# Normalizing two tiles on ScalarE in the head and issuing the next block's x loads earlier, in a fused layernorm, state-space and MLP kernel

## The chip, the cores and the metric

One core of a Trainium2 chip. The metric is the device time of one execution in microseconds (us). Each execution also records the span of the core (first to last instruction, about 1.3 us less than the time) and the clock granted to TensorE. All ratios here are the mean time of one kernel's fast runs over that of the other's fast runs of the same rounds, so not quite the ratio of the medians that are quoted. Runs of one call share a chip, and only runs of one call are compared directly unless the text says so.

## The reference, cut to what matters

```python
x  = A_x                                   # [1, 2048, 1024] bf16
xn = layernorm(x)                          # no gain, no bias, eps 1e-5
y  = 2 * Re(C @ scan(Lam_bar, xn @ B_bar)) + xn * Dskip      # 1024 complex states
h  = xn @ w1 + b1                          # w1 [1024, 3584]
z  = (h * tanh(softplus(h))) @ w2          # w2 [3584, 1024]
out = x + y + z
```

## The kernel before

The sequence is cut into four blocks of 512 rows. Each block runs 28 tiles of 128 columns of w1 (numbered 0 to 27 here, eight matmuls each), then the B projection, then a tail with w2 and C. A recording layer notes what each instruction reads and writes and makes the waits; each engine executes its own list in order. In the code PE, VE, AC and PO stand for the lists of TensorE, VectorE, ScalarE and GpSimd, SP for the sync queue, on which most transfers are issued; `mv` holds the mean of a row, `root(q)` one over its standard deviation, and GF is 7. Tile f uses PSUM bank f mod 8, so tile f waits until VectorE has evicted tile f - 8; the B projection starts with banks 4 and 5, those of tiles 20 and 21.

In block 0 the first seven tiles ("raw" tiles) start before x is normalized: rows 0 to 255 go in raw, and the normalization is applied to the product afterwards (`raw_scale`, `raw_add`). Rows 256 to 511 are normalized and transposed first, and `first_rest` (L558) adds them. Weights come through a ring of seven slots of half a K each:

```python
def first_apply(q):                        # normalize 128 rows, all four on VectorE
    vop(lambda e: e.tensor_scalar(xn[:, q, :], xx[:, 0, q, :], mv[:, q, 0:1], root(q),
                                  op0=ALU.subtract, op1=ALU.mult), ...)
...
for f in range(4): first_raw(f, 0, NK // 2)          # PE order of the head
first_spread()                                       # (a transpose of the parameters before it)
for f in range(4): first_raw(f, NK // 2, NK)         # needs the second weight load, "w1" below
...                                                  # statistics of rows 256.. on VectorE
first_sqrt(3)
first_raw(4, 0, NK // 2); first_raw(5, 0, NK // 2)
first_transpose(2); first_copy(2, AC)                # square root of 3 is AHEAD of this copy
first_raw(4, NK // 2, NK); first_raw(5, NK // 2, NK)
...
first_apply(3); first_transpose(3); first_copy(3, VE)
first_raw(6)
...
turns()
for j in range(NJ):                        # GpSimd: eight phases, about 5 us each
    phases(j)
    if j == 3:
        for q in range(NQ):
            load_x(PO, 1, q)               # x of block 1, four loads of 256 KB from GpSimd's queue
...
def first_tile(blk, f):                    # [cut: the eight matmuls]
    if f % 4 == 3:
        item_done(); item_done()           # two weight loads on the sync queue
    if f % GF == 0 and f >= 2 * GF:
        mish_mul(f // GF - 2)              # VectorE, L730: act * hb, 128 x 3584
    vop(...)                               # VectorE, L754: evict the tile
...
if f in (14, 16, 18, 20):                  # block 0, after the tile's eviction
    ln_stats_only(1, (f - 14) // 2)        # VectorE, L449: statistics of block 1's x
if f < 24 and f % 3 == 2:
    transpose_B(f // 3)                    # two transposing DMAs on the sync queue
```

## Time and profile before

| | before |
|---|---|
| median of three timed runs | 620.77 us (620.4 to 621.11) |
| the run whose profile was taken | 623.69 us, span 622.36 |
| TensorE matmul busy | 616.7 us, 99% |
| VectorE busy | 468.1 us, 75% |
| largest TensorE wait after the start-up | 1.8 us, first matmuls of the B projection (L767), for VectorE's eviction |
| VectorE's wait for block 1's x | 3.3 us in two pieces |

In the lines of the profile, here and in the prediction, PE is TensorE's matmuls, PEld its weight loads, DVE VectorE, ACT ScalarE, POOL GpSimd and SPq the issue of a transfer on the sync queue; a line of a timeline gives the start, the duration, the instruction and, in brackets, how long the engine had been idle and what ended that. How to read the rest: the share of busy time says only that TensorE is full; what can be won is in the gaps between its matmuls, and for each gap one asks which wait ends it. The lines are in the prediction. The changed kernel has line numbers about five higher (L754 becomes L759, L767 becomes L772, L449 becomes L454, L730 becomes L735).

### The profile page before, as it was taken

The numbers are of one execution on the slowest core, as the hardware profiler recorded it, in microseconds if no ns is written. First come the engines' busy times: TensorE is split into PE (matmuls) and PEld (weight loads), VectorE is DVE, ScalarE is ACT, GpSimd is POOL, SyncE is SP. The second block draws the span as 40 slices with busy tenths as digits, with TensorE's granted clock in tenths as the row PEclk, the third lists the DMA queues.
The fourth block names the chain that finished last, engine by engine and source line by source line (L and its number), as shares of the span: only waits on it lengthen the run. The fifth ranks groups of instructions, "written<-read, shape, count | busy, mean of one in ns | idle before, by whom it ended". The sixth has DMA issues, their size and how long they took to land.

```text
span 622.4 us, 7428 instructions
## 1 busy us (share of the span) xinstructions
PE 616.7 (99%) x2959; PEld 288.3 (46%) x2959; DVE 468.1 (75%) x698; ACT 248.1 (40%) x161; POOL 54.5 (9%) x57
## 2 busy tenths in 40 slices
PE   8998999999999999999999999999999999999998
PEld 7643444444444444444444444444444444444444
DVE  6988999999557599999047759999624856999603
ACT  4589997332069950000008992000000999000000
POOL 2899200000100000000010000000000000000000
DMA  9999995850355400774054430276302541033001
GB/s 230 298 263 280 224 145 176 199 167 0 117 173 174 144 2 9 218 185 131 11 188 138 135 136 1 73 203 173 93 35 101 164 174 69 1 119 118 1 0 68
DMA packets 97918, 79.94 MB, mean 128 GB/s; under 512 B 51035, under 2 KB 80347, under 8 KB 97883
## 3 DMA queue, kind: packets, MB, share of 16 engines
q1 hardware_dynamic: 94384, 72.17, 41.4%
q0 software_dynamic: 960, 3.15, 1.8%
q10 hardware_dynamic: 2538, 4.14, 1.8%
q8 instruction: 24, 0.39, 0.3%
q14 instruction: 12, 0.09, 0.1%
HBM read 63.19 MB, written 4.19 MB: 108 GB/s over the span
## 4 chain that ended last, share of the span: by engine, by line
PE 90%; POOL 4%; DMA 2%; DVE 2%; issue 1%; SPq 0%; POOLq 0%; DVEq 0%
PE ps L825 49%; PE ps L745 23%; PE ps L767 18%; DMA xx<-in_A_x_dram 2%; POOL py L627 1%; POOL px L625 1%; POOL ph_h L629 1%; DVE stats L449 1%; POOL rb L568 1%; DVE hb L754 1%; DVE act L730 0%; PE ps L839 0%; DVE stats L371 0%; SPq L310 0%; SPq L343 0%
## 5 line engine op out<-in xcount | busy, mean ns | idle before, releaser
L825 PE MATMUL ps<-ring,act 128*128 128x512 bf16 x896 | 194.0, 379 | 0.0
L745 PE MATMUL ps<-xnT,ring 128*128 128x512 bf16 x840 | 182.1, 379 | 0.0
L723 ACT ACTIVATE act<-hb 128x3584 bf16<-128x3584 bf16 x16 | 50.9, 3183 | 220.6 <-DVE hb L754 220.1
L825 PEld LDWEIGHTS ps<-ring,act 128*128 128x128 bf16 x896 | 87.7, 98 | 105.7
L745 PEld LDWEIGHTS ps<-xnT,ring 128*128 128x128 bf16 x840 | 82.1, 98 | 99.2 <-DVE hb L754 0.7
L754 DVE TENSOR_SCALAR hb<-ps,par 128x512 bf16<-128x512 f32 (+1 forms) x112 | 80.0, 730 | 52.6 <-PE ps L745 51.7
L767 PE MATMUL ps<-xnT,BT 128*128 128x512 bf16 x512 | 111.3, 379 | 1.8 <-DVE hb L754 1.8
L825 PE MATMUL ps<-CT,hT 128*128 128x512 bf16 x506 | 109.9, 379 | 0.0
L772 DVE TENSOR_TENSOR mt<-ps,tab 128x1024 bf16<-128x1024 f32 x64 | 75.4, 1219 | 13.3 <-PE ps L767 11.7
L767 PEld LDWEIGHTS ps<-xnT,BT 128*128 128x128 bf16 x512 | 50.0, 98 | 62.5 <-DVE hb L754 2.3
L825 PEld LDWEIGHTS ps<-CT,hT 128*128 128x128 bf16 x506 | 49.5, 98 | 59.7
L790 DVE TENSOR_TENSOR_SCAN hT<-cs,qi,hT 128x512 bf16<-128x512 f32 x48 | 58.9, 1269 | 0.0
L870 DVE TENSOR_TENSOR xx<-ps,xx 128x1024 bf16<-128x1024 f32 (+1 forms) x16 | 18.8, 1190 | 45.6 <-PE ps L825 45.6
L725 ACT ACTIVATE act<-act 128x3584 bf16<-128x3584 bf16 x16 | 51.1, 3191 | 0.2
L724 ACT ACTIVATE act<-act 128x3584 bf16<-128x3584 bf16 x16 | 51.0, 3190 | 0.2
L795 DVE TENSOR_TENSOR mt<-hT,tab 128x1024 bf16<-128x1024 bf16 x64 | 41.4, 688 | 1.1
L730 DVE TENSOR_TENSOR act<-act,hb 128x3584 bf16<-128x3584 bf16 x16 | 34.0, 2127 | 1.3 <-ACT act L725 1.3
L310 POOL DMA_DIRECT2D xx<-in_A_x_dram x12 | 6.7, 562 | 250.2 <-DVE xx L870 245.8
L699 ACT ACTIVATE ct<-CT,cs 128x512 f32<-128x512 bf16 x16 | 11.5, 720 | 26.3 <-DVE CT L701 25.9
L725 ACT ACT_TABLE_LOAD x16 | 20.5, 1283 | 0.3
L724 ACT ACT_TABLE_LOAD x16 | 20.5, 1283 | 0.3
L449 DVE BATCH_NORM_STATS2 stats<-xx 128x6 f32<-128x512 bf16 x24 | 16.3, 679 | 3.7 <-DMA xx<-in_A_x_dram 3.3
(101 smaller groups left out, 297.9 us busy)
## 6 DMA issues: line engine op xcount, KB each, us to landing
ring<-in_B_w_dram SPq DMA_DIRECT2D x112, 512.0 KB, 4.1
out_dram<-xx ACTq DMA_DIRECT2D x15, 256.0 KB, 2.0
xx<-in_A_x_dram POOLq DMA_DIRECT2D x12, 256.0 KB, 4.2
xx<-in_A_x_dram SPq DMA_DIRECT2D x3, 256.0 KB, 4.7
xx<-in_A_x_dram SPq DMA_DIRECT2D x2, 128.0 KB, 2.3
dsk<-in_A_Dskip_dram SPq DMA_DIRECT2D x1, 256.0 KB, 5.1
xnT<-xn SPq DMA_TRANSPOSE x14, 4.5
BT<-in_A_B_re_dram SPq DMA_TRANSPOSE x8, 5.8
```

Of the source, the lines that this page charges most:

```text
L449: vop(lambda e, h=h: e.bn_stats(stats[:, s, h, :], xx[:, i, q, h * 512:(h + 1) * 512]), reads=[b_xx[i][q]], writes=[b_stats[s]])
L723: aop(lambda e: e.activation(a, hs, AF.Exp), reads=[b_hb[g % 2]], writes=[b_act[g]])
L724: aop(lambda e: e.activation(a, a, AF.Ln, bias=1.0), reads=[b_act[g]], writes=[b_act[g]])
L725: aop(lambda e: e.activation(a, a, AF.Tanh), reads=[b_act[g]], writes=[b_act[g]])
L730: vop(lambda e: e.tensor_tensor(a, a, hs, op=ALU.mult), reads=[b_act[g], b_hb[g % 2]], writes=[b_act[g]])
L745: PE.mm(lambda e, k=k, w=w: e.matmul(ps[:, bank, :], lhsT=w, rhs=xnT[:, k, :], start=k == 0, stop=k == NK - 1), reads=[b_ring[s]] + b_xnT, ...
L754: vop(lambda e: e.tensor_scalar(hb[:, hs, ts], ps[:, bank, ts], b1(f), None, op0=ALU.add), reads=[b_ps[bank], b_par], writes=[b_hbf[hs]])
L767: PE.mm(lambda e, j=j, ci=ci, k=k, bank=bank: e.matmul(ps[:, bank + ci, :], lhsT=BT[:, ci, j, k, :], rhs=xnT[:, k, :], start=k == 0, stop= ...
L772: vop(lambda e, s=s, u=u, j=j: e.tensor_tensor(mt[:, s, :, :], u, tab[:, s, j, :].unsqueeze(1).to_broadcast([P, 2, TB]), op=ALU.mult), rea ...
L790: vop(lambda e, ci=ci, init=init: e.tensor_tensor_scan(out=hT[:, ci, j, :], data0=cj("r", j).to_broadcast([P, TB]), data1=hT[:, ci, j, :], ...
L795: vop(lambda e, s=s: e.tensor_tensor(mt[:, s, :, :], hT[:, :, j, :], tab[:, s, j, :].unsqueeze(1).to_broadcast([P, 2, TB]), op=ALU.mult), ...
L825: PE.mm(lambda e: e.matmul(ps[:, u, :], lhsT=lhsT, rhs=rhs, start=st_, stop=last), reads=reads, writes=[b_ps[u]], first=st_, last=last)
```

## The change

Two changes joined. First, in the head, the normalization of rows 0 to 255 moves from VectorE to ScalarE (their transposes into xnT are not needed before tile 7), the raw tiles 4, 5 and 6 run all first halves and then all second halves, the transpose of the parameters moves behind the second halves of tiles 0 to 3, tile 2's copy is cut in two, and one more weight load is issued at once. Second, the x loads of block 1 are issued after phase 1 instead of phase 3, so that VectorE does not wait for them.

```diff
     def first_apply(q):
+        if q < 2:
+            aop(lambda e: e.activation(xn[:, q, :], xx[:, 0, q, :], AF.Identity,
+                                       bias=rr[:, 2 + q:3 + q], scale=root(q)), ...)
+            return
         vop(lambda e: e.tensor_scalar(xn[:, q, :], ...
 ...
     def bank_T(q, k):
-        if q < 2 and k >= NK // 2:
-            return 4 + q
-        return 6 + q % 2
+        if q < 2:
+            return 4 + q + 2 * (k < NK // 2)
+        return 7
 ...                                        [cut: sign of the column sums, csum for ncs]
     first_scale(2)
     first_apply(2)
     first_sums_v(3, 1)
     first_var_v(3)
+    first_transpose(2)
+    first_copy(2, AC, 0, 4)
     first_sqrt(3)
-    first_raw(4, 0, NK // 2)
-    first_raw(5, 0, NK // 2)
-    first_transpose(2)
-    first_copy(2, AC)
-    first_raw(4, NK // 2, NK)
-    first_raw(5, NK // 2, NK)
+    first_copy(2, AC, 4, NK)
     raw_scale(0)
+    for f in range(4, NR):
+        first_raw(f, 0, NK // 2)
     first_scale(3)
     first_apply(3)
     first_transpose(3)
     raw_scale(1)
     first_copy(3, VE)
-    first_raw(6)
+    for f in range(4, NR):
+        first_raw(f, NK // 2, NK)
+    for q in range(2):
+        transpose_dma(q)                   [moved here; the fifth weight load now goes ahead of it]
 ...
     for j in range(NJ):
         phases(j)
-        if j == 3:
+        if j == 1:
             for q in range(NQ):
                 load_x(PO, 1, q)
```

## The prediction

> **What bounds the kernel now.** I first read the page's busy shares, then the waits, then the chain that ended last in order of time, then two stretches of the timeline: 7 to 17 us (the head) and 40 to 66 us (where the chain changes hands). Page of the kernel before:
>
> ```profile
> PE 616.7 (99%) x2959; PEld 288.3 (46%) x2959; DVE 468.1 (75%) x698; ACT 248.1 (40%) x161; POOL 54.5 (9%) x57
> ...
> PE   8998999999999999999999999999999999999998
> PEld 7643444444444444444444444444444444444444
> DVE  6988999999557599999047759999624856999603
> ```
>
> TensorE matmuls fill 99% of the span, so only a gap between matmuls can be won. Which gaps exist:
>
> ```profile
> DVE stats L449 <- DMA xx<-in_A_x_dram: 3.3, 2, 2.5
> ...
> PE ps L767 <- DVE hb L754: 1.8, 1, 1.8
> ...
> PEld ps L549 <- DMA ring<-in_B_w_dram: 1.1, 2, 0.7
> ...
> PEld ps L745 <- DVE hb L754: 0.7, 2, 0.5
> ```
>
> Apart from the start-up these are the only TensorE waits worth the name: one big one where the B projection (L767) begins, and small ones in the head. Chain that ended last, in order of time:
>
> ```profile
> 42.16 0.69 POOL xx L310
> 42.85 8.25 DMA xx<-in_A_x_dram
> 51.10 0.02 issue
> 51.12 0.71 DVE stats L449
> ...
> 58.48 2.96 DVE act L730
> ...
> 61.54 0.76 DVE hb L754
> ...
> 62.35 26.07 PE ps L767 x120
> ```
>
> Until 62.35 us the end is set by other engines: GpSimd's phases, the load of the next block's x, VectorE. From 62.35 to the end it is TensorE nearly without break; going through the starts of its matmuls I find none that starts more than 0.24 us after the one before. So the time is "when does matmul 9 of L767 start" plus a constant 560 us. The stretch 40 to 66 us:
>
> ```profile
> 47.41 1.43 DVE L449 BATCH_NORM_STATS2 stats<-xx 128x6 f32<-128x512 bf16 x2 [2.51 <-DMA xx<-in_A_x_dram]
> ...
> 58.40 3.03 DVE L730 TENSOR_TENSOR act<-act,hb 128x3584 bf16<-128x3584 bf16 x1
> ...
> 61.54 4.70 DVE L754 TENSOR_SCALAR hb<-ps,par 128x512 bf16<-128x512 f32 x7
> ```
>
> VectorE, in program order, sits idle 2.51 and then 0.78 us for x, falls behind, and evicts tile 21 (bank 5) only at 61.54 to 62.29. TensorE's matmul before the gap starts at 60.17, the next at 62.35: 2.18 us against a normal pitch of 0.216, a loss of 1.96. Another 0.15 is lost at 53.10 (tile 25 waiting for the eviction of tile 17). Head:
>
> ```profile
> 7.76 5.81 SPq L489 DMA_TRANSPOSE xnT<-xn  x2
> ...
> 11.79 0.55 DVE L383 TENSOR_SCALAR xn<-xx,mv,rs 128x1024 bf16<-128x1024 bf16 x1
> ...
> 13.22 0.29 ACT L379 ACTIVATE rs<-mv,kon 128x1 f32<-128x1 f32 x1 [2.54 <-DVE ncs L564]
> ...
> 13.74 0.55 DVE L383 TENSOR_SCALAR xn<-xx,mv,rs 128x1024 bf16<-128x1024 bf16 x1
> 13.96 1.01 ACT L412 COPY xnT<-ps 128x1024 bf16<-128x1024 bf16 x1 [0.45 <-PE ps L401]
> ```
>
> Here the square root of tile 3 (13.22) runs before the copy of tile 2 (13.96); the change swaps them.
>
> **What the Trainium skill says.** "Perfetto Trace Analysis", section Optimization Strategy: take the regime, find the gaps of its most-contended engine and what they wait for. That is the reading above, and the trace supports it. "ScalarE: Activation LUTs", section What ACT_TABLE_LOAD costs: an ACTIVATE with immediates takes 186 ns + 0.833 ns per element, each [128,1] pointer operand adds about 93 ns. The trace agrees: 1039 ns by the formula, 1012 measured for the 1024-wide copy. So a ScalarE normalization, with two pointers, is estimated at 1.23 us, where VectorE took 0.55. The same page, section Table sets, says that identity is in every set; the instruction listings have 40 ScalarE entries with a table load before and 40 after, so no load is added. "DMA: Bandwidth & Descriptors", section Queues, rings and completion order: each DMA engine consumes descriptors in ring order. The trace agrees in the head: issue order x1, w0, x2, w1, x3, w2, w3 lands at 5.24, 6.67, 7.33, 10.26, 10.97, 12.36, 13.77. A fifth weight load issued behind w3 should delay none of these.
>
> **The change, part by part.**
>
> *x loads two phases sooner.* GpSimd issues the four loads after phase 1 (its end is at about 31.3) instead of after phase 3 (42.1): 10.8 us sooner. The first two landed 5.3 and 9.0 us after the issue began (47.4, 51.1), so I expect about 37 and 41. VectorE asks first at 44.89, then after one tile's statistics and two evictions, 1.64 + 1.36 = 3.0 us later, at 47.9. Both idle times, 3.29 us, go. Tile 21 is then evicted by 62.29 - 3.29 = 59.0. TensorE would reach it, without gaps, at 58.66 - 0.15 + 8 x 0.216 = 60.24: slack 1.2 us, so both losses go whole, 1.96 + 0.15 = 2.1 us, and 1.2 us of VectorE's gain is worth nothing. GpSimd's total work, and so the end of phase 7 (66.3), stays.
>
> *The head.* Two normalizations (2 x 0.55 us) leave VectorE; this gains it nothing, as its next statistics of tile 3 wait for x3 (10.97) in either version, and the normalization of tile 2 ends at 12.34 as before. TensorE does the same matmuls in another order: raw at 0.112 us pitch, transposes at 0.056. Second halves of tiles 0 to 3 begin with w1 at 10.31 again and end at 12.10; the parameter transpose to 12.2; transposes of tile 2 wait for 12.34, so start at 12.39 and leave at 12.90; twelve first-half matmuls (12 x 0.112) end at 14.25. ScalarE starts half of tile 2's copy 0.25 after its last transpose, at 13.03; the square root of tile 3 follows 0.48 later (the pitch of the 512-wide copies in the head), at 13.51, against 13.22. Reciprocal and normalization follow at the old distances (+0.33, +0.20, +0.55): xn of tile 3 at 14.58, and its transposes start at 14.64, a gap of 0.39. They leave at 15.15; twelve second-half matmuls end at 16.5. VectorE's copy of tile 3 runs 15.28 to 15.97 and is hidden. So L558, the remainder of the raw tiles, starts at 16.5, against 16.11: a **loss of 0.4 us**. The order saves the old waits for w2 (0.30) and for the copy (0.06) and puts a wait for tile 2 (0.2) and one for tile 3 (0.39) in their place, besides small shifts.
>
> *The two transposes by DMA and the fifth weight load.* xn of tile 1 comes from ScalarE at about 11.7 instead of 8.8, so I estimate landings at 17 to 19 instead of 16.15 and 17.0. They are needed at tile 7, 22.6: hidden. w4 comes sooner, needed at 24: hidden.
>
> Sum: 2.1 - 0.4 = 1.7 us. From 62.35 on nothing changes: 620.77 - 1.7 = 619.1.
>
> **Rivals.**
> 1. *The head gains.* VectorE freed and w3 undisturbed by the transposes might bring TensorE's remainder forward to 15.8. For it: two waits of the old head do vanish. Against it: x3 and w1 fix 10.31 and 12.34 regardless. It would give 618.4.
> 2. *The gap of 1.96 turns into another wait,* since VectorE has 1.2 us of slack: tile 21's eviction stands behind the 3.03 us multiplication L730, which needs ScalarE's tanh (50.45 + 3.19 = 53.64). VectorE reaches it at 55.1, so it is not held. If the loads came later than I think (DMA is saturated here, busy share about 1.1), half of the gap would stay: 620.
> 3. *Contention.* 1 MB earlier on full DMA engines delays weight tiles or B's transposes. A weight slot is issued about 10 us before use and lands in 4.1, so 3 us more does no harm. If it did: 621.
> 4. *The DMA transposes of tiles 0, 1 land after 22.6.* Then TensorE waits at tile 7; the margin is some 4 us. It would give 620 to 622.
>
> **Range and chances.** The x gain is bounded by 2.1 (measured gaps); the head by about +-0.5 around -0.4; runs scatter by +-0.35. So 619.1, 8 times in 10 within 618.3 to 620.1. Two per cent is 12.4 us; nothing in this change reaches that: within 2% 0.99, faster 0.005, slower 0.005.
>
> **What would show it.** The VectorE wait on x (3.3) and the TensorE wait at L767 (1.8) gone from the waits; L767 all in one run from about 58.9; L558 starting at 16.5 (if at 16.1 or less, my head step is wrong); the square root of tile 3 at 13.5 and a TensorE gap near 14.3; x loads landing by 41; tile 21 evicted by about 59. Wrong if L767 still waits, if tile 7 waits for xnT, or if a weight wait appears between 22 and 60 us.

## The result, and the profile after

The changed kernel takes 621.35 us in the median (620.91 to 621.96, 6 runs), before 620.95 (620.4 to 621.67, 6 runs): ratio 1.0007, 95% interval 0.9994 to 1.002. It is the same within the scatter, and outside the predicted range of 618.3 to 620.1. Yet the profiled execution is 2.5 us shorter than the profiled execution of before, span 619.83 against 622.36.

The busy line of the changed kernel's page, then two of its waits (engine and line, for what, us in total, times, longest):

```profile
PE 613.3 (99%) x2903; PEld 288.4 (47%) x2959; DVE 466.1 (75%) x696; ACT 249.7 (40%) x164; POOL 55.0 (9%) x57
```

```profile
PEld ps L547 <- DMA ring<-in_B_w_dram: 0.3, 1, 0.3
...
PEld ps L750 <- DMA ring<-in_B_w_dram: 0.2, 1, 0.2
```

No wait for block 1's x and none at the B projection are left; a short wait for a weight tile (L750) is new. 56 matmul records of this trace are missing (2903 against 2959), so pitches are read from the weight loads (PEld), which are complete. The stretch 40 to 66 us, timeline:

```profile
43.90 1.41 DVE L454 BATCH_NORM_STATS2 stats<-xx 128x6 f32<-128x512 bf16 x2
...
54.01 2.22 DVE L735 TENSOR_TENSOR act<-act,hb 128x3584 bf16<-128x3584 bf16 x1
...
56.34 4.70 DVE L759 TENSOR_SCALAR hb<-ps,par 128x512 bf16<-128x512 f32 x7
...
58.09 8.15 PE L772 MATMUL ps<-xnT,BT 128*128 128x512 bf16 x36
```

VectorE starts the statistics without a wait, evicts tile 21 at 57.09 (56.34 plus one eviction) instead of 62.29, and L772 runs in one piece. Its head, timeline 7 to 23 us:

```profile
9.58 1.68 PEld L547 LDWEIGHTS ps<-xr,ring 128*128 128x128 bf16 x16 [0.29 <-DMA ring<-in_B_w_dram]
...
11.05 0.55 DVE L388 TENSOR_SCALAR xn<-xx,mv,rs 128x1024 bf16<-128x1024 bf16 x1
...
12.79 0.30 ACT L380 ACTIVATE rs<-mv,kon 128x1 f32<-128x1 f32 x1
...
13.32 0.55 DVE L388 TENSOR_SCALAR xn<-xx,mv,rs 128x1024 bf16<-128x1024 bf16 x1
...
13.92 0.45 PEld L406 LDWEIGHTS ps<-ident,xn 128*128 128x128 bf16 x8 [0.59 <-DVE xn L388]
...
15.61 6.10 PEld L556 LDWEIGHTS ps<-xnT,ring 128*128 128x128 bf16 x56
```

The second weight load (w1) is used from 9.58, where it was 10.30 in the profile before; and TensorE's weight loads wait 0.59 us for tile 3.

The two spans come apart into four terms. In every profile, 20 in all, the time from the first weight load of tile 7 to the end is 598.10 us plus the gaps of TensorE, to within 0.02 us (in e5 below a stretch at a lower clock comes on top). So span = (start on w1) + (from there to tile 7) + 598.10 + gaps:

| profile | start on w1 | to tile 7 | gaps after tile 7 | span |
|---|---|---|---|---|
| before | 10.30 | 11.83 | 2.13 | 622.36 |
| after | 9.58 | 12.15 | 0.00 | 619.83 |

The difference of -2.53 is -0.72 (w1 landed sooner), +0.32 (head) and -2.13 (gaps). The first was not part of the prediction (w1 is issued at 3.2 us in both kernels; "What stays open" comes back to it), and the last is worth something only if before has these gaps in its other runs too. The timed runs of before, at 620.4 to 621.67 us, have spans of about 619.1 to 620.4 and leave no room for 2.13.

### The profile page after: what moved, and what is told of

Read it like the earlier page. It is cut to its first block, busy times and chain, and to the rows that moved or that the text cites. A ratio compares the mean times of both kernels' runs of the same rounds, so it can differ in the third digit from the quotient of the medians.

```text
span 619.8 us, 7374 instructions
## 1 busy us (share of the span) xinstructions
PE 613.3 (99%) x2903; PEld 288.4 (47%) x2959; DVE 466.1 (75%) x696; ACT 249.7 (40%) x164; POOL 55.0 (9%) x57
## 3 DMA queue, kind: packets, MB, share of 16 engines
q0 software_dynamic: 960, 3.15, 1.9%
## 4 chain that ended last, share of the span: by engine, by line
PE 97%; DMA 1%; issue 1%; SPq 0%; DVE 0%; ACT 0%
PE ps L830 49%; PE ps L750 29%; PE ps L772 18%; DMA ring<-in_B_w_dram 1%; PE ps L556 1%; PE ps L547 1%; PE ps L844 0%; PE ps L406 0%; SPq L310 0%; SPq L314 0%; ACT xnT L417 0%; DVE xn L388 0%; SPq L343 0%; DVE xx L898 0%; ACT rs L380 0%
## 5 line engine op out<-in xcount | busy, mean ns | idle before, releaser
L750 PE MATMUL ps<-xnT,ring 128*128 128x512 bf16 x823 | 180.9, 379 | 0.9
L728 ACT ACTIVATE act<-hb 128x3584 bf16<-128x3584 bf16 x16 | 50.9, 3183 | 221.1 <-DVE hb L759 221.1
L750 PEld LDWEIGHTS ps<-xnT,ring 128*128 128x128 bf16 x840 | 82.2, 98 | 98.9 <-DMA ring<-in_B_w_dram 0.2
L772 PE MATMUL ps<-xnT,BT 128*128 128x512 bf16 x502 | 110.6, 379 | 0.5
L777 DVE TENSOR_TENSOR mt<-ps,tab 128x1024 bf16<-128x1024 f32 x64 | 75.4, 1219 | 15.2 <-PE ps L772 14.1
L772 PEld LDWEIGHTS ps<-xnT,BT 128*128 128x128 bf16 x512 | 50.1, 98 | 60.4
L730 ACT ACTIVATE act<-act 128x3584 bf16<-128x3584 bf16 x16 | 51.1, 3191 | 0.2
L735 DVE TENSOR_TENSOR act<-act,hb 128x3584 bf16<-128x3584 bf16 x16 | 32.5, 2034 | 2.6 <-ACT act L730 2.6
L795 DVE TENSOR_TENSOR_SCAN hT<-cs,hT 128x512 bf16<-128x512 f32 x16 | 18.7, 1208 | 0.0
```

What stands on the lines that cost most here:

```text
L728: aop(lambda e: e.activation(a, hs, AF.Exp), reads=[b_hb[g % 2]], writes=[b_act[g]])
L730: aop(lambda e: e.activation(a, a, AF.Tanh), reads=[b_act[g]], writes=[b_act[g]])
L735: vop(lambda e: e.tensor_tensor(a, a, hs, op=ALU.mult), reads=[b_act[g], b_hb[g % 2]], writes=[b_act[g]])
L750: PE.mm(lambda e, k=k, w=w: e.matmul(ps[:, bank, :], lhsT=w, rhs=xnT[:, k, :], start=k == 0, stop=k == NK - 1), reads=[b_ring[s]] + b_xnT, ...
L772: PE.mm(lambda e, j=j, ci=ci, k=k, bank=bank: e.matmul(ps[:, bank + ci, :], lhsT=BT[:, ci, j, k, :], rhs=xnT[:, k, :], start=k == 0, stop= ...
L777: vop(lambda e, s=s, u=u, j=j: e.tensor_tensor(mt[:, s, :, :], u, tab[:, s, j, :].unsqueeze(1).to_broadcast([P, 2, TB]), op=ALU.mult), rea ...
```

## The experiments

Theories. A: the gaps of 2.1 us were an accident of the one profiled run; the x loads win nothing in a usual run. B (rival): they are in every run of before, and the changed kernel pays as much elsewhere. C, formed after the second call: the stretch 22 to 62 us is at the limit of the DMA engines, and earlier x loads only move the risk of a late transfer from x to the weight tiles.

### First call: the four combinations, 5 rounds each

**e1_before_again**, no edit.

> The kernel before, unchanged, to see whether its profiled run was typical: that run took 623.69 us, 2.9 us over the median of its timed runs (620.77). Theory A (the 2.1 us TensorE gap before the B projection was mostly an accident of that one run, in which x landed late): the new profile has a span of 619 to 620.5 us and a gap at the B projection under 1 us. Theory B (the gap is in every run of before, and something in the changed kernel costs as much again): span about 622, or a gap of about 2 us within a shorter span.

**e2_x_only**, before with
```diff
-        if j == 3:
+        if j == 1:
```

> Only the x loads two phases sooner. Theory A: no gap to win, so within 0.5 us of before; and if the loads push B's transposes and weight tiles back (in the profile after, the second-half weight tile of 24 to 27 lands at 51.84 against 47.88), 0 to 0.5 us slower. Theory B, and my prediction: 2.1 us faster than before.

**e3_head_only**, the changed kernel with the reverse of that edit.

> Only the new head, x loads as before. My prediction's head step: 0.4 us slower than before (remainder of the raw tiles starts 6.14 us after the second weight tile lands, against 5.80). Theory A expects the same 0.3 to 0.5 us, that is all of the measured difference of the change. Rival (the head gains, the x loads lose): 0.3 us faster or more.

**e4_both_again**, the changed kernel, no edit.

> The changed kernel again, on the same chip. Theory A: the sum of the two single parts, +0.3 to +0.7 us over before. Theory B: equal to before with the gap gone and another of about 2 us present.

| label | median us | runs | ratio to before, 95% | start on w1 | to tile 7 | gaps | span |
|---|---|---|---|---|---|---|---|
| before of this call | 621.26 | 620.80 to 622.67, 9 | | | | | |
| e1_before_again | 620.88 | 620.63 to 621.86, 5 | 0.9995, 0.9983 to 1.0008 | 9.51 | 11.95 | 0 | 619.56 |
| e2_x_only | 621.15 | 620.42 to 622.09, 5 | 0.9996, 0.9984 to 1.0009 | 9.82 | 11.91 | 0 | 619.83 |
| e3_head_only | 621.39 | 620.99 to 621.96, 5 | 1.0000, 0.9986 to 1.0013 | 10.38 | 12.15 | 0 | 620.62 |
| e4_both_again | 621.25 | 620.48 to 621.42, 5 | 0.9995, 0.9982 to 1.0007 | 9.50 | 12.14 | 0 | 619.73 |

Second profile of before (e1_before_again), timeline 38 to 64 us:

```profile
46.13 1.42 DVE L449 BATCH_NORM_STATS2 stats<-xx 128x6 f32<-128x512 bf16 x2 [1.93 <-DMA xx<-in_A_x_dram]
...
56.25 1.97 DVE L730 TENSOR_TENSOR act<-act,hb 128x3584 bf16<-128x3584 bf16 x1
...
57.83 6.42 PE L767 MATMUL ps<-xnT,BT 128*128 128x512 bf16 x29
58.33 4.70 DVE L754 TENSOR_SCALAR hb<-ps,par 128x512 bf16<-128x512 f32 x7
```

VectorE still waits 1.93 us for x, but TensorE does not notice: tile 21 is evicted at 59.08, and TensorE, eight matmuls of 0.216 us after 57.83, wants its bank at 59.56. The slack is about 0.5 us. In the first profile x came later still, and a second thing followed from that: the multiplication L730 ran at 58.40 and took 3.03 us, here 1.97. There it started beside GpSimd's tensor_tensor (L629, 58.28 to 59.55). The Trainium skill, "SBUF — State Buffer", section SBUF: two separate sides, says that VectorE (with two SBUF inputs) and GpSimd share an exclusive port pair and the later of the two waits for the whole instruction; the 1.06 us of excess against 1.15 us of GpSimd's instruction still to go agree with that.

Theory A holds, B falls: e1 has no gap and its span is 619.56. e2 shows that the x part wins nothing that five runs could tell. My expectation of e4 as "+0.3 to +0.7 over before" is missed by the medians (-0.01), which the scatter allows; the head's cost is clear only inside the profiles, at 12.15 against 11.9.

### Second call: how close the cliff is, and the head's swap

**e5_x_late**, before with
```diff
-        if j == 3:
+        if j == 4:
```

> The kernel before with x issued after phase 4 instead of 3, so 5 us later. In the second profile of before VectorE waited 1.9 us for x and tile 21 was evicted at 59.1, 0.4 us before TensorE wanted its bank. If that small slack is the reason why nothing is won (Theory A), 5 us more of waiting go to TensorE almost whole: a gap of 4 to 5 us around the start of the B projection (part of it may show at tiles 23 to 25), and a time of about 625.5 us. If the load is hidden in some other way (rival: VectorE has far more slack than I read), the time stays under 622.

628.81 us (627.91 to 629.71, 4 runs), before of the call 620.63 (620.44 to 626.14, 7 runs), ratio 1.0112 (1.0068 to 1.0156): slower by more than the 625.5 expected, with an interval clear of 1, though by less than 2%. Timeline 40 to 62 us, and then two stretches of the table by windows (stretch, its length, busy us and count of PE, PEld, DVE, ACT, POOL, granted clock, DMA share, GB/s):

```profile
52.94 1.42 DVE L449 BATCH_NORM_STATS2 stats<-xx 128x6 f32<-128x512 bf16 x2 [8.87 <-DMA xx<-in_A_x_dram]
...
55.27 7.09 PE L745 MATMUL ps<-xnT,ring 128*128 128x512 bf16 x20 [6.06 <-DVE hb L754]
```

```profile
48.80:55.20 6.40, 0.41 (x2) 0.00 (x0) 2.19 (x5) 6.33 (x5) 6.20 (x6) 0.89 1.13 309
55.20:60.30 5.10, 5.03 (x12) 1.79 (x13) 4.96 (x11) 4.94 (x9) 4.83 (x4) 0.50 1.05 280
```

In the traces x was issued 6.6 us later than in e1 (47.97 against 41.41), not 5, and came 6.8 us later. The wait went to TensorE almost whole, as a gap of 6.23 us at tile 23. And something was missing in my sum: after that gap the granted clock was 0.50 for 5.1 us, in which 12 matmuls ran at twice the pitch, a further 2.6 us. This fits the records' mean clock of 0.995 in all four runs. The Trainium skill, "TensorE: Matmul & The Clock Gate", section The HAM clock gate, says that the array falls to half its clock after an idle window of about 3.4 us and is at full clock again after about 3.4 us of sustained work; the trace agrees with the halving, and here it lasted 5.1 us. I had not put it into the expectation. So VectorE's slack for x is what makes the load free in before, and it is short.

**e6_sqrt_first**, the changed kernel with
```diff
     first_transpose(2)
+    first_sqrt(3)
     first_copy(2, AC, 0, 4)
-    first_sqrt(3)
     first_copy(2, AC, 4, NK)
```

> The changed kernel with the square root of tile 3 ahead of both half copies of tile 2, as in before. If my head step is right that this swap delays tile 3, its transposes start 0.3 us sooner after the second weight tile lands, and tile 7 starts 11.85 us after the first matmul on that weight tile, against 12.15 in the three profiles with the new head and 11.83 to 11.95 in the three with the old one. Rival (the loss comes from elsewhere, such as the wait for tile 2): it stays at 12.1. In the time 0.3 us are within the scatter, so 620.4 to 621.6.

The runs are 622.01, 623.41, 626.77 and 627.51 us, ratio 1.0065 (1.0006 to 1.0124), so slower, against expectation. For the head the profile is clear, timeline 9 to 17 us:

```profile
13.22 0.29 ACT L380 ACTIVATE rs<-mv,kon 128x1 f32<-128x1 f32 x1 [0.43 <-DVE csum L562]
...
14.62 0.61 PE L406 MATMUL ps<-ident,xn 128*128 128x128 bf16 x8 [0.17 <-ACT xnT L417]
```

The square root is 0.4 us sooner after the start on w1 (2.80 against 3.21 us), but the transposes of tile 3 now wait for ScalarE's copy of tile 2: in the changed kernel both use bank 7 (`bank_T`). Tile 7 starts 12.00 us after the start on w1 instead of 12.15. So the swap is worth half of what I expected here (0.15 of 0.3 us), and less in the two later profiles with it (12.07 in e13, 12.11 in e18); in this profile the wait for the shared bank stands where the rest should be. The long runs are not in the head; they are taken up below.

**e7_before_look1** and **e8_before_look2**, before, one profile each.

> A third profile of before: Theory A expects a span of 619.3 to 620.7 and no gap over 0.5 us at the B projection; if the gap is there in half of all runs, about one of this and the next look shows it.

> A fourth profile of before, with the same expectation as the look before it.

621.94 us (span 620.70) and 620.85 us (span 619.52). e8 has no gap. e7 has none at the B projection, but one of 1.47 us at another place, tile 24; timeline 40 to 56 us:

```profile
44.56 5.51 SPq L710 DMA_TRANSPOSE BT<-in_A_B_re_dram  x1
...
52.92 3.41 PE L745 MATMUL ps<-xnT,ring 128*128 128x512 bf16 x14 [1.31 <-DMA ring<-in_B_w_dram]
```

The weight half of tiles 24 to 27 was issued at 43.2, while the x loads ran, and landed only at 52.87. So before has two tight places in this stretch, x and this weight half, and which of them comes late differs from run to run. This led to theory C. The slack of that half (landing to first use, from the traces' DMA landings):

| profile | slack us | gap at it |
|---|---|---|
| x late: before, e1, e3, e7, e8 | 4.4, 3.4, 0.6, late, 3.0 | 1.47 in e7 |
| x early: after, e2, e4 | late, 2.9, 1.9 | none counted; weight load waits 0.2 in after |
| x early, square root swapped: e6 | late | 0.16 |

In the changed kernel, moreover, the half of tiles 20 to 23 has 1.8 us of slack (7.4 in the first profile of before). The timeline 28 to 40 us of the changed kernel shows the x loads of GpSimd's queue meeting a transposition of B on the sync queue. The half of tiles 20 to 23, issued just ahead of both at 33.80, took 9.35 us to land (4.24 in the first profile of before); the half of tiles 24 to 27, behind the transposition, was issued only at 47.09 (41.98):

```profile
30.47 2.35 POOL L310 DMA_DIRECT2D xx<-in_A_x_dram  x4
...
34.93 6.58 SPq L715 DMA_TRANSPOSE BT<-in_A_B_re_dram  x1
```

### Third call: weight loads ahead of one transposition

The edit of the three shifted kernels, in the changed kernel (e10), in before (e11) and in e2's kernel (e12):
```diff
-            if f < 24 and f % 3 == 2:
+            if f < 24 and f % 3 == 2 and f != 14:
                 transpose_B(f // 3)
+            if f == 15:
+                transpose_B(4)
```

**e9_both_third**, the changed kernel, no edit.

> The changed kernel once more, on whatever chip this is. Theory C: the earlier x loads do not remove the risk in the stretch 40 to 62 us but move it, from VectorE's wait for x to the weight tile of tiles 24 to 27 (second half), which landed 0.04 to 3.4 us ahead of its use in all profiles so far and late in three of them. Then this kernel is within 0.6 us of before, and its profile shows that tile landing at 49 to 53 us, with a slack under 2 us. Rival: the weight tile's lateness is rare, and only the new head (0.25 us) and scatter explain the result; then the slack is over 3 us.

> The changed kernel with B's fifth pair of transposes issued after the weight loads that tile 15 frees instead of before them. Theory C: the weight loads go out 2.5 to 4 us sooner (about 41 instead of 45 to 47), the tile lands by 47, its slack is over 3 us, no TensorE gap from tile 7 to the end; times 620.3 to 621.4 with little scatter, at or up to 0.4 us below the changed kernel. If the rival holds, there is no difference.

> The same shift in the kernel before. Theory C: the weight tile has 3 us more slack, but VectorE still waits 2 us for x and keeps only 0.4 us of slack at tile 21; 620.2 to 621.4, scatter as in before.

> Old head, x loads two phases sooner, and the shift: the candidate for the best version, as both tight spots then have slack and the head keeps its 0.25 us. Expected 620.1 to 621.0, no gap after tile 7; below before by 0.1 to 0.6 us, so hardly clear of the scatter of the second weight tile's landing (9.1 to 10.3 us in the profiles so far).

| label | median us | runs | ratio, 95% | slack of the half of tiles 24 to 27 | gaps |
|---|---|---|---|---|---|
| before of this call | 621.17 | 620.54 to 624.97, 11 | | | |
| e9_both_third | 620.92 | 620.54 to 621.63, 5 | 0.9993, 0.9972 to 1.0014 | 1.8 | 0 |
| e10_both_Bshift | 621.15 | 620.69 to 621.84, 5 | 0.9995, 0.9974 to 1.0016 | 4.6 | 0 |
| e11_before_Bshift | 627.58 | 623.56 to 629.53, 6 | 1.0086, 1.0055 to 1.0117 | 9.1 | 3.15 |
| e12_x_only_Bshift | 621.02 | 620.40 to 621.66, 5 | 0.9989, 0.9966 to 1.0013 | 0.6 | 0.63 |

e9 and e10 go as theory C says on the slack: the shift gives the weight half 2.8 us, and the time does not change, as it was in time before too. Two details of e10 were missed: the half landed at 47.94, not by 47, and the runs scatter no less than e9's. e12 has another gap, of 0.63 us, at the half of tiles 20 to 23. e11 missed its expectation by 6 us and says the most: weight loads that go out 2.5 us sooner meet the x loads of before, whose first then takes 8.3 us to land (4.7 in e1), VectorE's wait for x grows to 5.5 us, and TensorE loses 3.15 us in the profiled run, the fastest of the six. Timeline 38 to 68 us:

```profile
49.31 1.42 DVE L449 BATCH_NORM_STATS2 stats<-xx 128x6 f32<-128x512 bf16 x2 [5.48 <-DMA xx<-in_A_x_dram]
...
51.65 8.81 PE L745 MATMUL ps<-xnT,ring 128*128 128x512 bf16 x40 [2.66 <-DVE hb L754]
```

The edit also puts the shifted transpositions beside these x loads (issued at 40.65 and 41.94), so whether the weights or the transpositions hold x up is not separated. In e11 and e12 what went sooner was paid for elsewhere in the stretch; in e10 no price is to be seen.

### Fourth and fifth calls: where the long runs come from

**e13_sqrt_first2** and **e14_both_fourth**, the kernels of e6 and after; **e15_x_only2** and **e16_before_again2**, the kernels of e2 and before.

> The square-root swap once more. In its first call, on a chip where before also had a run of 626 us, it had runs of 623.4, 626.8 and 627.5. Theory C (such runs come from DMA traffic of the chip in the stretch 40 to 62 us, not from the swap, which changes nothing there): on this chip it stays within 0.4 us of the changed kernel of the same call. Rival (the swap itself brings them): runs over 623 again, while the changed kernel has none.

> The changed kernel beside it. 620.3 to 621.8; first matmul of tile 7 12.14 us after the first on the second weight tile, as in its three profiles so far; sum of gaps under 0.3 us.

> Old head with the early x loads, the candidate that should beat both in the mean if the x part removes the rare long runs and the head part costs 0.2 us: 620.2 to 621.5, none over 622.2; tile 7 11.9 us after the second weight tile.

> The kernel before as a kernel of its own, for a fifth profile and five more runs: median 620.6 to 621.3, and by the 4 runs in 41 over 622.5 so far, about one such run among these five and the baseline's runs of the call.

| label | median us | runs | ratio, 95% |
|---|---|---|---|
| before of this call | 620.76 | 620.40 to 622.71, 11 | |
| e13_sqrt_first2 | 625.83 | 620.45, 620.60, 625.71 to 626.33 (4) | 1.0052, 1.0019 to 1.0085 |
| e14_both_fourth | 621.22 | 620.88 to 621.48 (5), 627.15 | 1.0019, 0.9990 to 1.0048 |
| e15_x_only2 | 620.67 | 620.33 to 621.00 (5), 625.41 | 1.0007, 0.9983 to 1.0031 |
| e16_before_again2 | 620.54 | 620.40 to 622.14, 5 | 1.0002, 0.9985 to 1.0018 |

The profile of e13 fell on a long run (span 625.01), timeline 28 to 62 us:

```profile
36.39 10.03 SPq L715 DMA_TRANSPOSE BT<-in_A_B_re_dram  x1
...
47.87 6.59 PEld L750 LDWEIGHTS ps<-xnT,ring 128*128 128x128 bf16 x32 [3.29 <-DMA ring<-in_B_w_dram]
...
57.22 4.86 PEld L750 LDWEIGHTS ps<-xnT,ring 128*128 128x128 bf16 x24 [2.75 <-DMA ring<-in_B_w_dram]
```

A transposition of B blocks the sync queue for 10.03 us while x comes in (its four loads landed between 38.9 and 46.4). The weight half of tiles 20 to 23, issued ahead of it at 33.76, takes 14.1 us to land, that of tiles 24 to 27 is issued only at 51.81; both come late, and TensorE loses 2.96 and 2.42 us. That is the kind of loss theory C speaks of, in a kernel with early x loads. But what theory C expected of e13, times within 0.4 us of the changed kernel, is missed: four of its six runs are long against one of six of e14, which is nearer to the rival (the swap brings them). The expectation that early x loads have no long runs is missed too: e14 and e15 have one each. The fifth profile of before, e16, has no gap and 0.46 us of slack at the half of tiles 24 to 27.

**e17_x_on_sync**, the old head, x of block 1 on the sync queue:
```diff
-        if j == 3:
-            for q in range(NQ):
-                load_x(PO, 1, q)
 ...
+            if f in (6, 8, 10, 12):
+                load_x(SP, 1, (f - 6) // 2)      # with semaphores of their own
```

> Old head; the next block's x is no longer loaded by GpSimd but in four single loads on the queue of the weights and of B's transposes, spread over tiles 6 to 12, so that its order among them is fixed and no second queue competes. Theory C (the risk in the stretch 22 to 62 us is the competition of two queues for the DMA engines, by which either x or a weight tile comes late): no transposition of B takes over 5 us to issue, the weight tiles of 20 to 23 and 24 to 27 land 2 us or more ahead of use, x ahead of VectorE; all runs within 620.2 to 622.2, no long one. Also VectorE's first product L730 takes 2.0 us and not 2.7, as GpSimd issues no load beside it. Rival (DMA is simply full there): a weight tile comes late in some runs, over 623.

**e18_sqrt_first_xold**, the kernel of e6 with the x loads back after phase 3.

> The new head with the square-root swap, x loads as late as in before. If the long runs of the swapped kernel (7 of 10 over 623) need the early x loads to collide with B's transposes and the weights, they are gone here or rare (at most 1 of 5) and the median is 620.6 to 621.6. If the swap itself brings them, 3 or more of 5 are over 623.

e17: 620.40 us, five runs from 620.39 to 620.75; before of the call 620.93 (620.41 to 622.71, 9 runs), ratio 0.9995 (0.9982 to 1.0007). No transposition in that stretch takes more than 3.93 us to issue and there is no gap after tile 7. This is from its timeline, 22 to 58 us:

```profile
47.09 3.93 SPq L708 DMA_TRANSPOSE BT<-in_A_B_im_dram  x1
```

Two details were missed: the half of tiles 24 to 27 has 1.35 us of slack, not 2, and the first multiplication (L728 there) still takes 2.71 us, so GpSimd's load issue is not what stretches it: in the trace it starts at 40.24 beside GpSimd's tensor_tensor (39.80 to 41.07), and the 0.74 us over 1.97 are near the 0.83 us which that had still to go. Its five runs scatter least of all kernels tried; its mean is not shown to be lower than before's, and five runs cannot show that long runs, 6 in 66 of before, are gone. Two things change at once in e17, the queue and the times of issue (26.7 to 41.0 us, where before has 41 to 44), so which of them counts is not separated.

e18: 621.36 us, 621.11 to 622.52, 5 runs, ratio 1.0010 (0.9996 to 1.0023). No run over 623, as expected if the swap needs the early loads; its profile has a gap of 1.47 us at the same weight half (landing late, beside a transposition of 6.8 us), so the tight place is there with late x too. It also has one of 0.22 us at the B projection, for VectorE's eviction, after VectorE waited 3.6 us for x: the path that I predicted, small.

All runs together, over all calls and chips: over 622.5 us are 6 of 66 runs of before, 1 of 22 of the changed kernel, 1 of 11 of e2's kernel, 7 of 10 of the swapped kernel with early x, 1 of 5 without (622.52), and none of 5 each of e3, e10, e12 and e17. The mean of the runs under 622.5 us is 621.02 for before and 621.20 for the changed kernel.

**What stays open**: why the swap, which acts at 13 us, makes the collision at 36 us so much more frequent when x is early. A small shift between the two queues is the obvious thought; no run shows it. Also open is what the clock adds to the long runs: of the ten runs over 624.5 us outside e5 and e11, eight show a mean granted clock of 0.997, and none of these eight was profiled. Last, w1 lands anywhere between 8.96 and 10.32 us and moves every kernel here by about 1 us. On average it landed at 9.39 in the eleven profiles with the old head and at 9.81 in the nine with the new one, later in each of the five calls of experiments. The new head issues a fifth weight load at 5 to 7 us, which the prediction held harmless. Whether it delays w1, and so adds to what the new head costs, no run shows: none takes it out alone, and w1 scatters by as much among the profiles of one head.

## Why the prediction was wrong

**The step that failed** is "both losses go whole, 1.96 + 0.15 = 2.1 us", together with "620.77 - 1.7 = 619.1". The gap was read from a run of 623.69 us and subtracted from the median of other runs, 620.77 us, that did not contain it. Four further profiles of before have 0, 1.47, 0 and 0 us of gaps after tile 7, none of it at the B projection. In place of 2.1 the term is 0 in a usual run: VectorE waits 1.7 to 2.3 us for the first x load in those profiles, and its slack takes that up at the B projection. Had I put the profiled run into my own sum, 623.69 minus 1.7, I would have been at 622 and seen that the base and the gap do not belong together.

**The mechanism of the x part** was right. The waits on x vanish in every profile with the early loads; in the changed kernel's first profile the loads landed at 35.6 to 41.6 (predicted 37 and 41 for the first two, by 41 for all; the first two came at 35.6 and 37.4). Tile 21 was evicted there at 57.09, sooner than the predicted 59.0: the two multiplications L735 took 2.02 and 2.22 us instead of 2.71 and 3.03, as they hardly overlap with GpSimd's tensor_tensor, and tile 7 had started 0.4 us earlier. e5 shows the path from the other side: later x goes to TensorE nearly one to one.

**The head** had the right sign and was a little too big: predicted 0.4, measured 12.15 against 11.83 to 11.95 in the five profiles of before, so 0.2 to 0.3 (the other kernels with the old head lie between 11.49 and 11.94, those with the new one between 12.14 and 12.17, the swapped ones aside). The steps in detail hold: from the start on w1 to the square root 3.20 predicted, 3.21 measured; to the transposes of tile 3, 4.33 and 4.35; to the remainder of the raw tiles, 6.19 predicted, 6.14 by matmul starts. What was off is the base: 5.80 us to the remainder in the first profile, where others of before have 5.8 to 5.9.

**The rival that I set aside** was contention: "a weight slot is issued about 10 us before use and lands in 4.1, so 3 us more does no harm". The 4.1 was a median over the whole kernel. In this stretch the second halves of tiles 20 to 27 took 4.2 to 14.1 us from issue to landing over all profiles, and the sync queue was blocked for up to 10.0 us by one transposition. The early loads push two weight halves to the edge in the changed kernel's first profile, and one of the prediction's own signs of being wrong, a weight wait between 22 and 60 us, stands there: 0.2 us at 51.88. In most runs nothing is lost by it, in some 5 us or more.

**The rest**: the two transposes by DMA landed at 17.05 and 17.94 (predicted 17 to 19), the ScalarE normalization took 1.24 us (estimated 1.23), no table load was added. The range was drawn from the scatter of the timed runs and from the head alone; the doubt about the base was not in it.

## What to carry to other kernels

Before a gap in a profile is priced, compare the time of the profiled run with the timed runs: a gap larger than the room between them is not in the usual run, and a second profile costs little. Where a stretch is full on several sides (here VectorE, PSUM banks and DMA), moving one transfer earlier can buy slack for one and take it from the next; write down the slack of each before and after. And loads that compete can be put in one queue, where their order is chosen: with it, and with other times of issue, five runs lay within 0.36 us here, though the mean is not shown to be lower.

## What the Trainium skill lacked or had wrong

- "Perfetto Trace Analysis", section Optimization Strategy, sends the reader from the gap to its cause, but not to the question whether the profiled run is a usual one. Here the profiled run took 623.69 us against a median of 620.77, and its gap of 1.96 us was in one of five profiles of the same kernel.
- "DMA: Bandwidth & Descriptors", section Queues, rings and completion order, has the round robin between queues, but nothing on how the issue of a transposing DMA stretches when another queue brings 1 MB: 1.2 us at best, 6.58 us and 10.03 us beside the x loads, and the loads behind it on the sync queue are issued later (5.1 us in the changed kernel's first profile). That the x loads cause it is argued from the overlap in time; with x on the same queue (e17) the longest was 3.93 us.
